# Two score blocks put side by side between matmuls of the second product, and one more tile of the first product in the values' buffers

## The chip, the cores and the metric

The kernel runs on one core of a Trainium2 chip. The metric is the device time of one execution in microseconds (us). Runs of this kernel differ among themselves by a few tenths of a microsecond.

## The reference

Attention with a few sink positions and a sliding window, followed by a two-layer network with a sigmoid-approximated gelu on the attention's output. Batch 4, 8 heads, 768 positions, 64 elements a head; 4 sinks, a window of 128; the network goes from 512 to 2048 and back to 512.

```python
scores = scale * np.matmul(q, k.transpose(0, 1, 3, 2))
keep = is_sink | in_window            # pos < n_sink, or 0 <= rel < window
scores = np.where(keep, scores, -1000000000.0)
scores = scores - np.max(scores, axis=-1, keepdims=True)
a = np.exp(scores)
a = a / (np.sum(a, axis=-1, keepdims=True) + 1e-09)
attn_out = np.matmul(a, v)
x = attn_out.transpose(0, 2, 1, 3).reshape(B * S, H * D)
h = x @ w_in
g = h * (1.0 / (1.0 + np.exp(-1.702 * h)))
out = g @ w_out
```

## The kernel before

**Tiles.** The 3072 rows of `x` are 12 groups of 256 (NG = 12, three to a batch entry). For a group, attention runs over four pairs of heads (hp = 0 to 3). The first product (`hidden`) makes the 2048 hidden features of a group in eight tiles (F2 = 0 to 7) of 256 features each, transposed, with 8 matmuls a tile; a gelu on ScalarE writes each into `gT`. The second product (`o`) makes a group's two blocks of 128 rows with 16 accumulating matmuls each.

**Attention of one group n.** `scores(n, hp)` writes the products of queries and keys (the previous 128 keys and the own 128, two heads, two blocks of rows) into a tile `nat`, with eight matmuls that use 64 rows of the array each. `maxima(n, hp)` on VectorE merges the two halves under the window's mask (L236), reduces to the row maximum (L240) and folds the sinks' maximum in (`bias`, L244). `weights` on ScalarE takes four exponentials (L255). `weights_transposed` turns them round: from group 3 on with a transposing DMA on the SP queue. `lower` (VectorE, L305) and `upper` (POOL, `affine_select`, L318) cut the transposed weights to the window; `values` multiplies with v into a tile `av`, and `normal` divides (L361, L362) into `xn`. The sinks have their own small path: `sinks`, `sink_terms` (L281, the tile `ts`), `sink_weights` (L290), `sink_transposed` (`tAs`, then the copy to `AsT`, L297). `x_transposed` turns `xn` to `xT` with a DMA.

**Accumulators.** All matmul results go to a pool with three tags. `nat` has two buffers, for scores. `mm` has two (`mm_bank`), for the hidden tiles `hT` and the `o` blocks. `av` has two (`av_bank`), for `tAs`, the sinks' scores `sk`, the values `av`, and hT of F2 = 2 and 3 in the one group g = NG - 2. Buffers of a tag are handed out in turn, and a tile waits until the tile two before it of the same tag has been read.

**The order.** The order on each engine is that of the program text (a manual schedule); each engine works its own queue in order and waits on semaphores. The loop at L665 runs n = 2 to 13, and one pass is called a stage here. In stage n, attention of group n is finished, the scores of group n + 1 begin, the first product runs for group n - 1 and the second for group n - 2. A stage first calls `second`, then goes through F2 = 0 to 7: after hT1 come `sink_transposed(n)`, the sinks and the first two pairs' scores and maxima of group n + 1 (`ahead`); after later tiles come the four `values` and `normal`.

In `second`, the first two pairs' weights go to ScalarE, then TensorE runs the first `o` block (16 matmuls), the third pair's scores, four matmuls of the second block, the fourth pair's scores, and the other twelve. `out_store(g2, 0)` copies the first block on ScalarE (L435), `out_store(g2, 1)` the second on VectorE (L437), and each store is issued on the SP queue (L439). VectorE's order in this part: third pair's maxima, fourth pair's maxima, `ts`, the L437 copy, then `lower` of the first pair, `AsT`, the sinks' values, and so on. SP's: the first two pairs' transposes, the first block's store, the third pair's transpose, the second block's store, the fourth pair's transpose, and the transpose of the queries and keys of group n + 2. POOL's: `upper` of the four pairs, with loads of group n + 3 issued between and after them; v's loads are paced by `rcp` tiles (`paced_load`).

Of the kernel before, what the change touches and what calls it, by code (L numbers as in the profile page):

```python
# [57 lines left out]
def kernel(  # L58
# [18 lines left out]
    NF = DF // P  # L77
    NT = S // TG
    NG = B * NT
# [23 lines left out]
    def mm_bank(name, shape=(P, 512), dt=FP32):  # L103
        return psp.tile(list(shape), dt, tag="mm", bufs=2, name=name)
# [66 lines left out]
    def sink_keys(b: int, copy):  # L171
        kT = G[b * NT]["qkT"]
        for h in range(2):
            copy(
                out=kd[b][bass.ts(h, D), :, bass.ts(h, n_sink)],
                in_=kT[bass.ts(h, D), 1, 0, :, 0:n_sink],
            )
# [31 lines left out]
    def scores(g: int, hp: int):  # L209

        b, t = divmod(g, NT)
        qkT = G[g]["qkT"]
        nat = psp.tile([P, 2, 2, 2 * P], FP32, tag="nat", bufs=2, name=f"nat{g}_{hp}")
        for i in range(2):
            I = 2 * t + i
            prev = None if I == 0 else qkT[:, 1, 0, hp] if i else G[g - 1]["qkT"][:, 1, 1, hp]
            for part, keys in ((0, prev), (1, qkT[:, 1, i, hp])):
                for h in range(2):
                    r = bass.ts(h, D)
                    o = nat[:, h, i, bass.ts(part, P)]  # L220
                    if keys is None:
                        nc.tensor.matmul(o, masked_l[r], masked_r[r], start=True, stop=True)
                    else:
                        nc.tensor.matmul(o, qkT[r, 0, i, hp], keys[r], start=True, stop=True)  # L224
        G[g]["nat", hp] = nat

    def kinds(mask, t: int):

        m = mask.rearrange("p (i c) -> p i c", i=2)
        if t == 0:  # L230
            return m.unsqueeze(1).broadcast_to((P, 2, 2, P))
        return m[:, 1:2].unsqueeze(1).broadcast_to((P, 2, 2, P))

    def maxima(g: int, hp: int):
        nat = G[g]["nat", hp]
        nc.vector.copy_predicated(  # L236
            out=nat[:, :, :, P:], mask=kinds(take_prev, g % NT), data=nat[:, :, :, 0:P]
        )
        m1 = work.tile([P, 2, 2], FP32, tag="m1", name=f"m1{g}_{hp}")
        nc.vector.tensor_reduce(  # L240
            out=m1.rearrange("p h i -> p (h i)"), in_=nat.rearrange("p h i c -> p (h i) c")[:, :, P:],
            axis=AX.X, op=ALU.max,
        )
        nc.vector.scalar_tensor_tensor(  # L244
            out=G[g]["bias"][:, :, hp], in0=m1.rearrange("p h i -> p i h"), scalar=-scale,
            in1=G[g]["m2"][:, :, hp], op0=ALU.mult, op1=ALU.min,
        )

    def weights(g: int, hp: int):

        nat, bias = G[g]["nat", hp], G[g]["bias"]
        A = work.tile([P, 4, P], FP16, tag="A", bufs=4, name=f"A{g}_{hp}")
        for h in range(2):
            for i in range(2):
                nc.scalar.activation(  # L255
                    out=A[:, 2 * h + i], in_=nat[:, h, i, P:], func=AF.Exp, bias=bias[:, i, hp, h : h + 1],
                    scale=scale,
                )
        G[g]["A", hp] = A

    def weights_transposed(g: int, hp: int):
        A = G[g]["A", hp]
        AT = work.tile([P, 2, 2, P], FP16, tag="AT", bufs=6, name=f"AT{g}_{hp}")
        flat = AT.rearrange("p h i s -> p (h i) s")
        if g < 3:
            bank = av_bank if g == 2 or (g, hp) == (1, 3) else mm_bank
            tp = bank(f"tA{g}_{hp}", (P, 4, P), FP16)
            for a in range(4):
                nc.tensor.transpose(tp[:, a], A[:, a], ident)
            if g == 0 or hp < (2 if g == 2 else 3):  # L270
                nc.scalar.copy(flat, tp)
            else:
                nc.vector.tensor_copy(out=flat, in_=tp)
        else:
            nc.sync.dma_start_transpose(flat, A.rearrange("p a c -> p (a c)"))
        G[g]["AT", hp] = AT
# [10 lines left out]
    def sink_weights(g: int):  # L287
        ts_ = G[g]["ts"]
        As = sinkA[g % 2]
        nc.scalar.activation(out=As[:, 0:64], in_=ts_.rearrange("p a j -> p (a j)"), func=AF.Exp)  # L290
        G[g]["As"] = As
# [92 lines left out]
    def hidden(g: int, F2: int):  # L384
        xT = G[g]["xT"]
        if F2 == 0:
            G[g]["gT"] = work.tile([P, NF, TG], FP16, tag="gT", bufs=3, name=f"gT{g}")

        bank = av_bank if g == NG - 2 and F2 in (2, 3) else mm_bank
        hT = bank(f"hT{g}_{F2}", (P, 2, 2, P))  # L390
        for f in range(2):
            F = 2 * F2 + f
            for c in range(4):
                nc.tensor.matmul(  # L394
                    hT[:, f], w_in16[:, c, bass.ts(F, P)], xT[:, :, c], start=(c == 0), stop=(c == 3)
                )
        nc.scalar.activation(  # L397
            out=G[g]["gT"][:, 2 * F2 : 2 * F2 + 2].rearrange("p f s -> p (f s)"),
            in_=hT.rearrange("p f i s -> p (f i s)"),
            func=AF.Gelu_apprx_sigmoid,  # L400
        )

    def out_part(g: int, i: int, part: int):

        if part == 0:
            G[g]["o", i] = mm_bank(f"o{g}_{i}")
        o, gT = G[g]["o", i], G[g]["gT"]
        for F in range(4 * part, 4 * part + 4):
            nc.tensor.matmul(o, gT[:, F, bass.ts(i, P)], w_out16[:, F], start=(F == 0), stop=(F == NF - 1))  # L409

    def out_last(g: int, i: int):

        b, t = divmod(g, NT)
        gT, r = G[g]["gT"], b * S + t * TG + i * P
        osb = work.tile([P, DM], FP32, tag="osb", bufs=3, name=f"osb{g}_{i}")
        for half in range(2):
            c = bass.ts(half, DM // 2)
            o = mm_bank(f"o{g}_{i}_{half}", (P, DM // 2))
            for F in range(NF):
                nc.tensor.matmul(o, gT[:, F, bass.ts(i, P)], w_out16[:, F, c], start=(F == 0), stop=(F == NF - 1))  # L420
            if half == 0:
                nc.scalar.copy(osb[:, c], o)
                nc.sync.dma_start(out[r : r + P, c], osb[:, c])
            else:
                d, a = bass.ts(2, P), bass.ts(3, P)
                nc.vector.tensor_copy(out=osb[:, d], in_=o[:, 0:P])
                nc.sync.dma_start(out[r : r + P, d], osb[:, d])
                nc.scalar.copy(osb[:, a], o[:, P:])
                nc.scalar.dma_start(out[r : r + P, a], osb[:, a])

    def out_store(g: int, i: int):
        b, t = divmod(g, NT)
        osb = work.tile([P, DM], FP32, tag="osb", bufs=3, name=f"osb{g}_{i}")
        if i == 0:
            nc.scalar.copy(osb, G[g]["o", i])  # L435
        else:
            nc.vector.tensor_copy(out=osb, in_=G[g]["o", i])  # L437
        r = b * S + t * TG + i * P
        nc.sync.dma_start(out[r : r + P, :], osb)  # L439
# [54 lines left out]
    def o(g: int, i: int, *parts):  # L494
        if 0 <= g < NG:
            for p in parts:
                out_part(g, i, p)

    def valued(g: int, hp: int):
        values(g, hp)  # L500
# [129 lines left out]
    def second(n: int, g2: int, att: bool):  # L630

        if att and n + 1 < NG and (n + 1) % NT == 0:
            sink_keys((n + 1) // NT, nc.gpsimd.tensor_copy)
        if att:
            for hp in (0, 1):
                weights(n, hp)
                weights_transposed(n, hp)
        o(g2, 0, 0, 1, 2, 3)
        if att:
            scores(n, 2)  # L640
            maxima(n, 2)
        if g2 == NG - 1:
            out_store(g2, 0)
            out_last(g2, 1)
            return
        o(g2, 1, 0)
        if att:
            scores(n, 3)
            maxima(n, 3)
            sink_terms(n)  # L650
        o(g2, 1, 1, 2, 3)
        out_store(g2, 0)
        if att:
            weights(n, 2)
            weights_transposed(n, 2)
        out_store(g2, 1)
        if att:
            weights(n, 3)
            weights_transposed(n, 3)
            sink_weights(n)  # L660
            lower(n, 0)
            if n + 2 < NG:
                transposed_qk(n + 2)

    for n in range(2, NG + LAG2):  # L665
        att = n < NG
        g1, g2 = n - LAG1, n - LAG2

        if n > 2:
            second(n, g2, att)  # L670
        else:
            transposed_qk(n + 2)
# [73 lines left out]
```

## Time and profile before

| what | value |
|---|---|
| median of 3 runs | 243.81 us (243.29 to 244.23) |
| the profiled execution | 243.37 us |
| its span, from the first to the last instruction | 241.5 us |
| busy: TensorE / VectorE / ScalarE / POOL | 222.7 / 146.1 / 156.1 / 104.7 us |
| granted TensorE clock over the span | 0.998 |

Stages of the profiled execution, each from its first `o` matmul:

| n | 2 | 3 | 4 | 5 | 6 | 7 | 8 | 9 | 10 | 11 | 12 | 13 |
|---|---|---|---|---|---|---|---|---|---|---|---|---|
| starts at, us | 43.57 | 62.70 | 79.56 | 96.84 | 114.63 | 131.46 | 148.74 | 166.12 | 182.94 | 200.59 | 216.90 | 230.92 |
| lasts, us | 19.1 | 16.9 | 17.3 | 17.8 | 16.8 | 17.3 | 17.4 | 16.8 | 17.7 | 16.3 | 14.0 | 10.6 |

Stages 3, 6 and 9 finish the first group of a batch entry, which has fewer matmuls in `values`. A row of the trace in order of time has the start in us from the span's start, the duration, engine, line, operation, output and inputs, shape, and a count of merged instructions; in brackets stands how long the engine was idle before it and what ended that. TensorE's durations include the time in its pipeline, so rows of matmuls overlap, and a step is better read from start to start. "DVE" is VectorE, "ACT" ScalarE, "PE" TensorE's matmuls, "PEld" its weight loads.

### The profile page before, as it was taken

How to read it: one execution, taken by the hardware profiler on the slowest of the kernel's cores; microseconds unless marked ns; L12 is line 12 of the kernel's file. 1: busy time of each engine (PE TensorE's matmuls, PEld its weight loads, DVE VectorE, ACT ScalarE, POOL GpSimd, SP SyncE). 2: the span in 40 equal slices, each digit the busy share in tenths (PEclk: the TensorE clock that was granted, in tenths of full speed). 3: DMA queues.
4: the chain of work that ended last, by engine and by line, in shares of the span. 5: the costliest groups of instructions: out<-in, count | busy, mean ns of one | idle time of the engine just before them, and what ended most of it. 6: DMA issues, size and time to landing. Idle time of an engine off the chain costs nothing.

```text
span 241.5 us, 5809 instructions
## 1 busy us (share of the span) xinstructions
PE 222.7 (92%) x2220; PEld 155.7 (64%) x2220; DVE 146.1 (61%) x389; ACT 156.1 (65%) x355; POOL 104.7 (43%) x158
## 2 busy tenths in 40 slices
PE   1656799999999999999999999999999999999994
PEld 0443678569658569478478487486585685684863
DVE  4688856488568378377667575586682893830100
ACT  2268693784866875785786776677668658760531
POOL 8977486847326447354438057058020310310000
PEclk9999999999999999999999999999999999999999
DMA  8999999999999999999999999999982513503102
GB/s 74 151 188 193 177 207 180 154 120 145 127 150 190 138 165 157 112 189 121 124 183 159 153 163 141 173 134 139 129 214 46 151 25 62 148 11 87 46 0 87
DMA packets 130699, 32.07 MB, mean 133 GB/s; under 512 B 123120, under 2 KB 127728, under 8 KB 130672
## 3 DMA queue, kind: packets, MB, share of 16 engines
q0 software_dynamic: 79104, 13.64, 78.9%
q1 hardware_dynamic: 50992, 17.88, 43.0%
q8 instruction: 17, 0.28, 0.5%
q10 hardware_dynamic: 576, 0.20, 0.3%
q14 instruction: 10, 0.08, 0.1%
HBM read 27.50 MB, written 6.29 MB: 140 GB/s over the span
## 4 chain that ended last, share of the span: by engine, by line
PE 63%; DVE 14%; ACT 13%; DMA 5%; issue 3%; POOL 1%; SPq 0%; ACTq 0%; DVEq 0%; POOLq 0%
PE hT L394 28%; PE o L409 22%; ACT A L255 6%; DVE m L240 5%; DVE nat L236 5%; ACT L397 3%; PE nat L224 3%; DMA AT<-A 2%; PE av L344 2%; DMA qkn<-in_k_dram 2%; ACT gT L397 2%; PE av L332 2%; PE av L340 2%; PE o L420 1%; DVE xn L362 1%
## 5 line engine op out<-in xcount | busy, mean ns | idle before, releaser
L394 PE MATMUL hT<-xT,w_in 128*128 128x256 f16 x768 | 95.1, 274 | 1.1 <-ACT gT L397 0.4
L409 PE MATMUL o<-w_out,gT 128*128 128x512 f16 x368 | 85.4, 380 | 0.0
L397 ACT ACTIVATE gT<-hT 128x512 f16<-128x512 f32 x96 | 56.1, 597 | 41.2 <-PE hT L394 40.9
L394 PEld LDWEIGHTS <-w_in 128*128 128x128 f16 x768 | 72.7, 98 | 13.4 <-issue 0.6
L318 POOL TENSOR_SCALAR_AFFINE_SELECT up<-AT 128x512 f16<-128x512 f16 (+1 forms) x48 | 27.8, 585 | 99.1 <-DMA AT<-A 91.7
L255 ACT ACTIVATE A<-nat,bias 128x128 f16<-128x128 f32 x192 | 53.7, 376 | 18.6 <-DVE bias L244 17.1
L409 PEld LDWEIGHTS <-gT 128*128 128x128 f16 x368 | 33.6, 98 | 37.2
L236 DVE COPY_PREDICATED nat<-prev,nat 128x512 f32<-128x512 uint16 x48 | 33.2, 692 | 28.7 <-PE nat L224 19.0
L240 DVE TENSOR_REDUCE m<-nat 128x4 f32<-128x512 f32 x48 | 33.2, 691 | 1.7
L123 POOL DMA_DIRECT2D vn<-in_v_dram x24 | 21.3, 898 | 3.4 <-DMA w_out<-in_moe_w_out_dram 2.3
L123 POOL DMA_DIRECT2D qkn<-in_k_dram x24 | 21.3, 894 | 2.5 <-DMA w_in<-in_moe_w_in_dram 2.0
L123 POOL DMA_DIRECT2D qkn<-in_q_dram x24 | 21.6, 910 | 1.3 <-POOLq L727 0.8
L305 DVE TENSOR_TENSOR lo<-AT,own 128x512 f16<-128x512 f16 (+1 forms) x48 | 18.2, 397 | 5.9 <-DMA AT<-A 5.7
L362 DVE TENSOR_TENSOR xn<-av,rcp 128x256 f16<-128x256 f32 x48 | 20.4, 424 | 1.7
L340 PE MATMUL av<-vn,up 128*128 128x65 f16 x160 | 18.4, 196 | 0.0
L344 PE MATMUL av<-vn,lo 128*128 128x65 f16 x160 | 18.3, 196 | 0.0
L332 PE MATMUL av<-vs,AsT 128*128 128x130 f16 x80 | 16.5, 224 | 0.6 <-DVE xn L362 0.3
L224 PEld LDWEIGHTS <-qkT 64*128 64x128 f16 x352 | 11.8, 100 | 7.7 <-issue 7.0
L224 PE MATMUL nat<-qkT 64*128 64x128 f16 x288 | 16.6, 232 | 0.0
L361 DVE RECIPROCAL rcp<-av 128x4 f32<-128x4 f32 x48 | 8.5, 178 | 12.3 <-PE av L344 12.0
L340 PEld LDWEIGHTS <-up 128*128 128x128 f16 x160 | 14.8, 100 | 1.4 <-POOL up L318 0.5
L397 ACT ACT_TABLE_LOAD x11 | 14.1, 1283 | 0.2
(58 smaller groups left out, 180.3 us busy)
## 6 DMA issues: line engine op xcount, KB each, us to landing
out_dram<-osb SPq DMA_DIRECT2D x23, 256.0 KB
qkn<-in_q_dram POOLq DMA_DIRECT2D x24, 128.0 KB, 5.6
qkn<-in_k_dram POOLq DMA_DIRECT2D x24, 128.0 KB, 5.4
vn<-in_v_dram POOLq DMA_DIRECT2D x24, 128.0 KB, 6.6
w_in<-in_moe_w_in_dram POOLq DMA_DIRECT2D x4, 512.0 KB, 10.4
w_out<-in_moe_w_out_dram POOLq DMA_DIRECT2D x4, 512.0 KB, 11.6
AT<-A SPq DMA_TRANSPOSE x36
xT<-xn SPq DMA_TRANSPOSE x10
```

What stands on the lines that cost most here:

```text
L123: nc.gpsimd.dma_start(dst, (q, k, v)[e][b, :, rows].rearrange("h s d -> s h d"))
L224: nc.tensor.matmul(o, qkT[r, 0, i, hp], keys[r], start=True, stop=True)
L236: nc.vector.copy_predicated(out=nat[:, :, :, P:], mask=kinds(take_prev, g % NT), data=nat[:, :, :, 0:P])
L240: nc.vector.tensor_reduce(out=m1.rearrange("p h i -> p (h i)"), in_=nat.rearrange("p h i c -> p (h i) c")[:, :, P:], axis=AX.X, op=ALU.max,)
L255: nc.scalar.activation(out=A[:, 2 * h + i], in_=nat[:, h, i, P:], func=AF.Exp, bias=bias[:, i, hp, h : h + 1], scale=scale,)
L318: nc.gpsimd.affine_select(out=out, in_=in_, pattern=[[0, rows], [-1, P]], compare_op=ALU.is_gt, fill=zero_reg, base=0, channel_multiplier=1,)
L340: nc.tensor.matmul(av[:, i, h], up[:, h, i], vn[b][J // 2][:, J % 2, head], start=False, stop=False)
L344: nc.tensor.matmul(av[:, i, h], own_w[:, h, i], vn[b][t][:, i, head], start=(I == 0), stop=(I == 0 or h == 1))
L362: nc.vector.tensor_tensor(out=G[g]["xn"][:, :, hp], in0=av[:, :, :, 0:D], in1=rcp.to_broadcast((P, 2, 2, D)), op=ALU.mult)
L394: nc.tensor.matmul(hT[:, f], w_in16[:, c, bass.ts(F, P)], xT[:, :, c], start=(c == 0), stop=(c == 3))
L397: nc.scalar.activation(out=G[g]["gT"][:, 2 * F2 : 2 * F2 + 2].rearrange("p f s -> p (f s)"), in_=hT.rearrange("p f i s -> p (f i s)"), fun ...
L409: nc.tensor.matmul(o, gT[:, F, bass.ts(i, P)], w_out16[:, F], start=(F == 0), stop=(F == NF - 1))
```

## The change

In `second`, both score blocks of the third and fourth pair now stand together, after the first two matmuls of the second `o` block; both maxima and `sink_terms` follow, then the other 14 matmuls. `out_part` takes a range of the 16 matmuls in place of a quarter, and the helper `o` is adapted to it. In `hidden`, the third tile (F2 = 2) of groups 2 to 9 (first product in stages 3 to 10) takes an `av` buffer, as F2 = 2 and 3 of group 10 did before and still do.

```diff
-        bank = av_bank if g == NG - 2 and F2 in (2, 3) else mm_bank
+        more = (2,) if 2 <= g < NG - 2 else (2, 3) if g == NG - 2 else ()
+        bank = av_bank if F2 in more else mm_bank
...
-    def out_part(g: int, i: int, part: int):
+    def out_part(g: int, i: int, F0: int, F1: int):
-        if part == 0:
+        if F0 == 0:
             G[g]["o", i] = mm_bank(f"o{g}_{i}")
         o, gT = G[g]["o", i], G[g]["gT"]
-        for F in range(4 * part, 4 * part + 4):
+        for F in range(F0, F1):
             nc.tensor.matmul(o, gT[:, F, bass.ts(i, P)], w_out16[:, F], start=(F == 0), stop=(F == NF - 1))
...
-                out_part(g, i, p)
+                out_part(g, i, 4 * p, 4 * p + 4)
...
         o(g2, 0, 0, 1, 2, 3)
-        if att:
-            scores(n, 2)
-            maxima(n, 2)
         if g2 == NG - 1:
             out_store(g2, 0)
             out_last(g2, 1)
             return
-        o(g2, 1, 0)
+        out_part(g2, 1, 0, 2)
         if att:
+            scores(n, 2)
             scores(n, 3)
+            maxima(n, 2)
             maxima(n, 3)
             sink_terms(n)
-        o(g2, 1, 1, 2, 3)
+        out_part(g2, 1, 2, NF)
         out_store(g2, 0)
```

## The prediction

> **What bounds the kernel now.** I read the page first, then the busy time by stage (a stage is one pass of the loop at L665, named by its n; it starts with the first `o` matmul of `second`), then the chain of waits through stage 6, then the rows of that stage in order of time.
>
> ```profile
> span 241.5 us, 5809 instructions
> PE 222.7 (92%) x2220; PEld 155.7 (64%) x2220; DVE 146.1 (61%) x389; ACT 156.1 (65%) x355; POOL 104.7 (43%) x158
> ...
> PE 63%; DVE 14%; ACT 13%; DMA 5%; issue 3%; POOL 1%; SPq 0%; ACTq 0%; DVEq 0%; POOLq 0%
> ```
>
> TensorE is the bound, but a fourth of the chain that ended last goes through VectorE and ScalarE. By stage (length, busy time of PE, PEld, DVE, ACT, POOL):
>
> ```profile
> 96.84:114.63 17.79, 17.37 (x183) 11.91 (x180) 11.46 (x29) 12.30 (x29) 8.02 (x13) 1.00 1.56 141
> 114.63:131.46 16.83, 16.75 (x171) 11.47 (x169) 11.67 (x30) 12.19 (x29) 9.19 (x17) 1.00 1.48 155
> ```
>
> The clock is full (1.00). Stage 6 (second row) is nearly all TensorE; stage 5 has 0.4 us of plain idle. Its detour, in the chain of waits (start, length, what):
>
> ```profile
> 114.79 3.45 PE o L409 x16
> ...
> 118.69 0.71 DVE nat L236
> 119.42 0.70 DVE m L240
> ...
> 120.23 0.70 DVE nat L236
> 120.95 0.70 DVE m L240
> ...
> 122.02 1.14 ACT A L255 x4
> ...
> 123.32 1.28 ACT L397
> 124.61 0.60 ACT gT L397
> ...
> 125.26 1.91 PE hT L394 x16
> ```
>
> The third pair's scores start two maxima on VectorE, the fourth pair's weights, a table load and the first gelu on ScalarE; the third tile of the first product (hT2) waits for that gelu, since it takes hT0's buffer. The same stretch in order of time:
>
> ```profile
> 118.18 0.23 PE L222 MATMUL nat<-maskedr,maskedl 64*128 64x128 f16 x2
> ...
> 118.51 1.04 PE L409 MATMUL o<-w_out,gT 128*128 128x512 f16 x4
> ...
> 119.48 0.23 PE L222 MATMUL nat<-maskedr,maskedl 64*128 64x128 f16 x2
> ...
> 119.81 2.77 PE L409 MATMUL o<-w_out,gT 128*128 128x512 f16 x12
> ...
> 121.88 0.23 DVE L281 TENSOR_TENSOR ts<-bias,sn 128x64 f32<-128x64 f32 x1
> ...
> 122.41 1.98 PE L394 MATMUL hT<-xT,w_in 128*128 128x256 f16 x16
> ...
> 122.61 0.69 DVE L437 COPY osb<-o 128x512 f32<-128x512 f32 x1 [0.51 <-PE o L409]
> ```
>
> A busy PE hides small losses, so I take steps from start to start in the single records. An `o` matmul steps 0.213 (twelve of them: 122.41 - 119.81 = 2.60), a set of eight 64-row score matmuls 0.21. On top, going from `o` to scores costs 0.10 and going back 0.12, twice a stage. hT1 waits 0.07 for L437 to end (123.30), since it takes that buffer; hT2 comes 0.27 after its step, of which 0.12 is the way back from scores and 0.15 the wait for the gelu (end 125.21, start 125.26). In stage 10 that wait is 0.51.
>
> **Part 1: the scores side by side.** Nothing is added or left out: 16 score matmuls, two maxima and 32 `o` matmuls stay. One round trip between `o` and scores goes: 0.10 + 0.12 = 0.22 on TensorE. Two sets with nothing between them show no gap in the rows of `ahead` (sets start at 124.56 and 124.79). But the third set now comes behind two matmuls of the second `o`: 2 x 0.213 = 0.43 later. Queued behind it on VectorE, in order: both maxima, `ts` and the L437 copy. VectorE idled 2.08 before the first maxima and runs without a gap from 118.69 to the end of `ts` at 122.11, so the fourth pair's maxima gain nothing from earlier scores and the whole run moves by 0.43: `ts` at 122.31 to 122.54. L437 doesn't depend on `ts`; independent neighbours on VectorE overlap by 0.08 (bias ends 120.32, the next nat starts 120.23), so it runs 122.46 to 123.15. It was bound by TensorE before (0.51 idle), by VectorE after. hT1 can start at 123.19; TensorE is there at 122.41 - 0.22 + 0.85 = 123.04 and waits 0.15 instead of 0.07. Of the 0.22, 0.16 reaches hT1 (123.35 before).
>
> The fourth set needs its `nat` buffer from weights(n, 1), whose last exponential ends 3.92 to 4.04 after the stage's start; the set comes at 3.55 + 0.43 + 0.21 = 4.19. No wait, with 0.10 to spare after 0.05 for the signal. ScalarE's weights move by 0.43, covered by its idle 1.46 and 0.39, and with them the SP queue: the third pair's transpose is issued at 7.49 instead of 7.06 into the stage, read by VectorE at 13.8; the fourth pair's, held by the output store before it on SP (issued 8.70, then 0.43), stays at 9.1, since the weights then end at 8.98. The store itself follows L437, 0.16 earlier. POOL's `up` of the third pair (9.7 to 10.5) may come some tenths later; its reader on TensorE is at 15.5.
>
> **Part 2: the third tile in a buffer of the values.** In stages 3 to 10 hT2 takes the `av` buffer that `AsT`'s copy frees, and waits for that (0.25 after `tAs`, before the scores end) in place of the gelu. It starts 0.12 after the scores: 10.48 - 0.16 = 10.32 into the stage instead of 10.63, a gain of 0.31. The first gelu is what is late next: 0.43 later it ends at 11.01, and hT3, which now takes hT0's buffer, comes at 10.32 + 0.85 = 11.17. So the cover is 0.12; a gelu later than that is paid in full. Stage 11 has this edit already.
>
> **What takes it back.** (a) The values. The fourth pair's `lo` stands before the first `rcp` and `xn` on VectorE, and the third `av` waits for that `xn`. Stage 5, where the transposed weights landed late:
>
> ```profile
> 112.02 0.43 DVE L305 TENSOR_TENSOR lo<-AT,own 128x512 f16<-128x512 f16 x1 [0.93 <-DMA AT<-A]
> ...
> 113.05 0.22 PE L332 MATMUL av<-vs,AsT 128*128 128x130 f16 x1 [0.34 <-DVE xn L362]
> ```
>
> From landing to `av` takes 113.05 - 112.02 = 1.03. With TensorE 0.31 earlier, `av` is wanted at 15.39 of the stage, so a landing after 14.37 costs its whole excess. Landings seen: 15.18 (stage 5), 14.77 (8), 14.34 (7), no wait in the others. Stages 5 and 8 thus gain 0.
>
> (b) VectorE can be held up by POOL:
>
> ```profile
> 207.72 0.63 POOL L318 TENSOR_SCALAR_AFFINE_SELECT up<-AT 128x512 f16<-128x512 f16 x1 [0.95 <-DMA AT<-A]
> ...
> 207.84 0.59 DVE L281 TENSOR_TENSOR ts<-bias,sn 128x64 f32<-128x64 f32 x1
> ```
>
> This `ts` took 0.59 instead of 0.23 and ended with the `up`. `ts`, `bias` and `lo` show this in 12 places, L437, nat and m in none. With `ts` at 7.67 to 7.90 of the stage, it meets the first `up`, which starts at 7.69, 7.80, 7.65 and 7.88 in stages 4, 5, 7 and 8. If `up` starts first, L437 moves by about 0.44 and that stage loses 0.13 instead of gaining 0.31. Stages 4 and 7 are nearest: one of the two, 0.18 between them, I take.
>
> The Trainium skill (SBUF — State Buffer, "Who interferes with whom") says that a VectorE instruction with two SBUF inputs contends with a GpSimd instruction that reads SBUF, and that whoever issues first blocks the other. The 0.59 row agrees; by this rule the delay of `ts` is a risk in every stage where an `up` starts near it, which rival 2 prices from rows.
>
> In stage 10, `up` at 5.63 to 6.26 meets the moved second-last `bias` (5.94; +0.17), while the 0.36 that the next `bias` lost before (189.99, 0.53 long) goes: hT2 at 10.50 instead of 10.99, 0.49 gained. In stage 11 both `bias` meet an `up` (+0.10, +0.21) less the 0.36 of `ts`: 0.
>
> **Sum.** Stages 3, 6, 9: 0.93. Stages 4 and 7: 0.18. Stages 5, 8 and 11: 0. Stage 10: 0.49. Together 1.6. The profiled execution took 243.37 (span 241.5 and 1.9 around it), 0.44 under the median 243.81; so 241.8 for it and 242.2 for the median.
>
> **Rivals.**
> 1. The late landings of 5 and 8 were chance: they gain 0.31 each like the others, `up` meets no `ts`, and stage 5's 0.51 stall goes. 1.6 + 0.62 + 0.44 + 0.5 = 3.2: 240.6; with half of it, 241.3. For: transfers of `q` (issued 8.97 and 9.05 in those stages) went just ahead of the transpose (9.14, 9.13), a matter of tenths. Against: three of nine stages show it.
> 2. `up` comes first in stages 4, 5, 7 and 8: 0.93 + 0.49 - 4 x 0.13 = 0.9 gained, 242.9. Against: the `up`s of 5 and 8 start well after `ts` begins.
> 3. Slower: the fourth pair's transposed weights land as late as 15.18 in stages 4 to 8, because transfers now stand closer together. `av` then comes at 16.21 instead of 15.70, 16.21, 15.47, 15.70 and 15.80: 0.51 + 0 + 0.74 + 0.51 + 0.41 = 2.2 lost, against 0.62 + 0.49 gained in 3, 9 and 10: 1.1 slower, 244.9. It decides from 14.37 on. For: stage 5. Against: the transpose is issued no later than before.
> 4. The change doesn't do what it says: the fourth set waits 0.2 for its `nat` buffer (cover 0.10). L437 then starts 0.1 later, nine times: 0.9 less, 243.1.
>
> **Chances.** Forecast 0.42; rival 1 0.24; rival 2 0.13; rival 3 0.13; rival 4 0.08. About 0.5% (1.2 us) is what a measurement of this kernel can tell from no change: faster needs under 242.6. The forecast gives 0.37 of its chance to that, rival 1 all, rivals 2 and 4 some 0.02 together: 0.63. Slower by over 1.2 is the half of rival 3 and what I can't see: 0.12. The rest, 0.25, is between. The range leaves out the far end of rival 1 and most of rival 3: 240.7 to 244.1.
>
> **What would show it.** Right: one pair of ways into and out of scores in `second`; the first maxima at 4.49 of the stage; L437 at 7.8 without idle time; hT2 0.12 after the last score set; stages 3, 6 and 9 shorter by 0.3. Wrong: hT3 waiting for the gelu, L437 starting after 8.2, `av` waiting for `xn` in more than stages 5 and 8, or an `up` side that stops TensorE.

## The result and the profile after

The changed kernel takes 242.24 us (median of 21 runs, 241.02 to 244.12), the kernel before 243.71 us (21 runs, 242.58 to 245.38). The ratio is 0.9944, with a 95% interval from 0.9925 to 0.9963: 1.5 us less between the medians. The forecast was 242.2. Single runs of one kernel spread over about 3 us here, not over the few tenths named at the start, so medians and intervals have to carry a difference of this size.

The page of the profiled execution (243.37 us before, span 241.5):

```profile
span 240.3 us, 5809 instructions
PE 220.8 (92%) x2220; PEld 155.9 (65%) x2220; DVE 145.3 (60%) x389; ACT 155.3 (65%) x355; POOL 104.4 (43%) x158
...
PE 78%; DVE 9%; DMA 5%; ACT 3%; issue 2%; POOL 1%; DVEq 0%; POOLq 0%
```

VectorE's and ScalarE's share of the chain that ended last fell from 27% to 12%. The busy time by stage, stages 4 to 7 and 9 (first to last time, length, then busy time of PE, PEld, DVE, ACT and POOL, and last the granted clock, the DMA engines' share and GB/s):

```profile
79.09:96.07 16.98, 16.98 (x182) 11.93 (x180) 11.08 (x29) 12.32 (x29) 8.67 (x14) 1.00 1.39 156
96.07:113.06 16.99, 16.99 (x183) 11.95 (x181) 11.32 (x29) 12.21 (x29) 10.01 (x18) 1.00 1.35 146
113.06:131.52 18.46, 16.57 (x170) 11.39 (x168) 11.67 (x30) 12.29 (x29) 7.99 (x15) 1.00 1.78 164
131.52:148.72 17.20, 17.03 (x183) 11.96 (x180) 11.20 (x29) 12.32 (x29) 8.06 (x13) 1.00 1.21 149
...
165.78:182.30 16.52, 16.52 (x170) 11.47 (x168) 11.68 (x30) 12.08 (x29) 4.46 (x9) 1.00 1.17 145
```

Against 17.28, 17.79, 16.83, 17.28 and 16.82 before, every one is shorter by 0.1 to 0.8, but for stage 6, which is 1.6 longer. Stages 3 to 11 together take 153.08 instead of 154.20. Stage 9 shows the change undisturbed. Its chain of waits (start, length, what) no longer leaves TensorE:

```profile
165.94 3.88 PE o L411 x18
169.83 0.16 PE nat L222 x2
169.99 0.17 PE nat L224 x6
170.16 0.06 PE nat L222 x2
170.21 0.17 PE nat L224 x6
170.38 3.13 PE o L411 x14
173.51 1.86 PE hT L396 x16
175.37 0.06 PE tAs L295
175.43 0.18 PE sk L195 x8
175.61 0.55 PE nat L224 x16
176.16 1.85 PE hT L396 x16
```

The detour over maxima, exponentials, a table load and the first gelu is gone. The same stage in order of time:

```profile
170.27 0.70 DVE L236 COPY_PREDICATED nat<-prev,nat 128x512 f32<-128x512 uint16 x1 [2.52 <-ACT osb L437]
...
173.46 0.23 DVE L281 TENSOR_TENSOR ts<-bias,sn 128x64 f32<-128x64 f32 x1
...
173.60 0.68 DVE L439 COPY osb<-o 128x512 f32<-128x512 f32 x1
...
176.09 1.37 PE L396 MATMUL hT<-xT,w_in 128*128 128x256 f16 x11
176.19 1.58 ACT L399 ACTIVATE gT<-hT 128x512 f16<-128x512 f32 x3
```

The stage starts at 165.78. The first maxima comes at 4.49 of it (4.06 before), the copy follows `ts` without a gap, and hT2 starts at 10.31, ahead of the first gelu (10.41). In stage 6 TensorE then waits for something else:

```profile
122.67 1.05 PE L396 MATMUL hT<-xT,w_in 128*128 128x256 f16 x8 [1.89 <-DMA xT<-xn]
```

The transposed `xT`, issued 0.88 into the stage, is there only at 9.6. It is wanted at 7.57, and was wanted at 7.78 before. The trace keeps 16 marks for the landing of such a transfer: here eight come at 7.80 to 7.88 of the stage and eight at 9.43 to 9.57. Between them, from 7.97 to 9.45, lies a pause of the transfers, in which 21 packets take 1.45 to 1.55 us each (the last section has more on pauses). In a second profile of this kernel (below) the same `xT` has landed at 5.88.

### The profile page after: what moved, and what is told of

Its sections match the earlier page's. It is cut to its first block, busy times and chain, and to the rows that moved or that the text cites. A ratio compares the mean times of both kernels' runs of the same rounds, so it can differ in the third digit from the quotient of the medians.

```text
span 240.3 us, 5809 instructions
## 1 busy us (share of the span) xinstructions
PE 220.8 (92%) x2220; PEld 155.9 (65%) x2220; DVE 145.3 (60%) x389; ACT 155.3 (65%) x355; POOL 104.4 (43%) x158
## 4 chain that ended last, share of the span: by engine, by line
PE 78%; DVE 9%; DMA 5%; ACT 3%; issue 2%; POOL 1%; DVEq 0%; POOLq 0%
PE hT L396 35%; PE o L411 27%; PE nat L224 4%; DMA xT<-xn 4%; DVE m L240 3%; DVE nat L236 3%; PE av L344 2%; ACT A L255 2%; PE av L340 2%; PE av L332 2%; DMA qkn<-in_k_dram 2%; PE tA L269 2%; PE o L422 1%; DVE xn L362 1%; PE tqk L152 1%
## 5 line engine op out<-in xcount | busy, mean ns | idle before, releaser
L411 PE MATMUL o<-w_out,gT 128*128 128x512 f16 x368 | 83.8, 379 | 0.0
L399 ACT ACTIVATE gT<-hT 128x512 f16<-128x512 f32 x96 | 55.4, 597 | 37.0 <-PE hT L396 36.8
L411 PEld LDWEIGHTS <-gT 128*128 128x128 f16 x368 | 34.3, 98 | 38.4
L224 PE MATMUL nat<-qkT 64*128 64x128 f16 x288 | 15.5, 232 | 0.0
```

The lines of the kernel that those rows point to most:

```text
L399: nc.scalar.activation(out=G[g]["gT"][:, 2 * F2 : 2 * F2 + 2].rearrange("p f s -> p (f s)"), in_=hT.rearrange("p f i s -> p (f i s)"), fun ...
```

## The experiments

All ratios are to the kernel before, run on the same chip, with 95% intervals.

### The parts apart: the scores' place alone, the third tile's buffer alone

```diff
 # side_only: the changed kernel, but
-        more = (2,) if 2 <= g < NG - 2 else (2, 3) if g == NG - 2 else ()
+        more = (2, 3) if g == NG - 2 else ()
 # buffer_only: the kernel before, but
-        bank = av_bank if g == NG - 2 and F2 in (2, 3) else mm_bank
+        more = (2,) if 2 <= g < NG - 2 else (2, 3) if g == NG - 2 else ()
+        bank = av_bank if F2 in more else mm_bank
```

> The scores stand side by side as in the changed kernel, but the third tile of the first product stays in an mm buffer. Theory (scores later by two o matmuls move VectorE's run and the first gelu by 0.43, and this tile waits for that gelu): the tile starts at 11.06 of the stage instead of 10.63 before, so 0.43 more in each of stages 3 to 9, 0.2 in stage 10, partly given back where a late landing made TensorE wait anyway; about 2.5 us slower than before, ratio 1.008 to 1.013. Rival (the saved way between o and scores, 0.16 to 0.22 a stage, is a gain by itself): 1.4 to 2.0 us faster, ratio about 0.993.

Measured: 247.54 us, ratio 1.0149 (1.0119 to 1.018), slower than either kernel. The mechanism is the one expected, in order of time (stage 6, starting at 116.56):

```profile
126.97 1.08 ACT L399 ACTIVATE gT<-hT 128x512 f16<-128x512 f32 x2
127.62 0.60 PE L396 MATMUL hT<-xT,w_in 128*128 128x256 f16 x4 [0.68 <-ACT gT L399]
```

hT2 waits for the gelu and starts at 11.06, to the hundredth as expected. The size was too small: in stages 4, 5, 8 and 10 an `up` on POOL held VectorE up as well, and hT2 came at 11.23 to 11.42.

> The scores stay where they were before; only the third tile of the first product of stages 3 to 10 takes an av buffer. Theory: the tile starts at 10.48 of the stage, 0.12 after the scores, instead of 10.63; 0.15 less in seven stages and 0.51 in stage 10, 1.6 us in all without late landings and 1.2 with them, ratio 0.993 to 0.996. Its profile shows no wait for the gelu. Rival (this buffer only passes the wait on to the next tile or the values): no change, ratio 0.998 to 1.002.

Measured: 242.04 us, ratio 0.993 (0.9902 to 0.9958). In order of time, stage 9 (starting at 165.57; line numbers are one lower than in the changed kernel):

```profile
175.55 1.09 ACT L398 ACTIVATE gT<-hT 128x512 f16<-128x512 f32 x2
...
176.05 1.16 PE L395 MATMUL hT<-xT,w_in 128*128 128x256 f16 x9
```

hT2 starts at 10.48, before the first of the two gelus ends (10.58), so the rival falls. And again, beside the changed kernel:

> The third tile's buffer alone. Theory (late transfers and hold-ups take from the side-by-side scores what they save): within 0.6 us of the changed kernel, ratio 0.992 to 0.996. Rival (the scores' place is worth 1.4 us with loads too): 243.6 us, ratio 0.999.

> The changed kernel, beside the two that follow. Theory: 242.2 us, ratio 0.994; its stages without a late transfer or a hold-up by POOL last 16.52 and 16.98.

Measured: the buffer alone 242.14 us, 0.9931 (0.9912 to 0.995); both parts 242.19 us, 0.9941 (0.9921 to 0.9961). hT2 starts at 10.48 with the buffer alone, undisturbed stages last 16.69 and 17.15, with both parts 16.52 and 16.98. The scores' place thus saves 0.17 in each undisturbed stage (0.11 in stage 11), 1.5 over nine stages, and nothing that the medians show. In the profiles, what stages 3 to 11 last beyond their undisturbed length is 2.4 and 2.2 us with both parts (two executions), and 0.7 and 1.3 with the buffer alone. Split by the rows, late transfers make 2.0 and 0.6 of it with both parts and 0.7 and 1.3 with the buffer alone. Hold-ups of VectorE by POOL make 0.4 and 1.5 with both parts, and 0 and 0.06 with the buffer alone.

One such loss in the second profile of the changed kernel, stage 4 (starting at 79.33), in order of time:

```profile
86.98 1.22 POOL L318 TENSOR_SCALAR_AFFINE_SELECT up<-AT 128x512 f16<-128x512 f16 x2 [5.49 <-DMA AT<-A]
87.01 0.67 DVE L281 TENSOR_TENSOR ts<-bias,sn 128x64 f32<-128x64 f32 x1
87.61 0.68 DVE L439 COPY osb<-o 128x512 f32<-128x512 f32 x1
...
88.34 0.38 PE L396 MATMUL hT<-xT,w_in 128*128 128x256 f16 x2 [0.40 <-DVE osb L439]
```

The first `up` starts 0.03 before `ts`; `ts` takes 0.67 instead of 0.23, the copy is late, and hT1 starts at 9.01 of the stage instead of 8.56. In stage 7 `bias` and `ts` are both held up (0.63 and 0.61 long, hT1 at 9.41), and in stages 5 and 8 the third `av` waits 0.11 and 0.46 for late `lo`.

### The scores later still

```diff
-        out_part(g2, 1, 0, 2)
+        out_part(g2, 1, 0, 4)
...
-        out_part(g2, 1, 2, NF)
+        out_part(g2, 1, 4, NF)
```

> The changed kernel with four instead of two matmuls of the second o block ahead of the two score blocks. TensorE does the same work with the same number of ways into and out of scores. Theory (VectorE's run from the first scores to the copy of the second o block sets when the second tile may start): the run moves by another 0.43, the copy starts at 8.25 of the stage, the second tile at 8.98 instead of 8.55 and the third at 10.75; about 0.43 a stage, 3.4 us slower than the changed kernel where nothing else is late, 1 us slower than the kernel before, ratio 1.002 to 1.007. Rival (only the number of ways between o and scores counts): as the changed kernel, ratio 0.994.

Measured: 246.13 us, ratio 1.0104 (1.0067 to 1.0141). In order of time, stage 6 (starting at 115.61):

```profile
123.72 0.23 DVE L281 TENSOR_TENSOR ts<-bias,sn 128x64 f32<-128x64 f32 x1
...
123.86 0.68 DVE L439 COPY osb<-o 128x512 f32<-128x512 f32 x1
124.59 0.60 PE L396 MATMUL hT<-xT,w_in 128*128 128x256 f16 x4 [0.38 <-DVE osb L439]
```

The copy at 8.25, hT1 at 8.99: VectorE's run decides, and the rival falls. The loss is above the range, since `ts` or a `bias` now meets an `up` in stages 4, 7, 8 and 11 (hT1 at 9.28 to 9.80).

### The copy ahead of `ts`

```diff
             maxima(n, 3)
-            sink_terms(n)
         out_part(g2, 1, 2, NF)
...
         out_store(g2, 1)
         if att:
+            sink_terms(n)
             weights(n, 3)
```

> The changed kernel with VectorE's copy of the second o block ahead of the tile ts. Theory: the copy starts at 7.76 of the stage, when o is done, instead of 7.82 and is no longer moved where POOL holds up ts; the second tile starts at 8.49 instead of 8.55; 0.06 in nine stages, 0.5 us less than the changed kernel, ratio to before about 0.992. Rival (the loss in these stages is late transfers, not VectorE): no difference from the changed kernel, 0.994.

> The changed kernel with the copy of the second o block ahead of ts. Theory: 0.5 to 1.0 us below the changed kernel, ratio 0.990 to 0.992. Rival (the first run of it was lucky with its transfers): as the changed kernel, 0.994.

Measured: 241.19 us, ratio 0.9909 (0.9875 to 0.9944), and 241.72 us, 0.9916 (0.9901 to 0.9932), the second beside 242.19 for the changed kernel. In order of time, stage 6 of the first:

```profile
121.49 0.16 DVE L244 SCALAR_TENSOR_TENSOR bias<-m,m 128x4 f32<-128x4 f32 x1
...
121.78 0.69 DVE L439 COPY osb<-o 128x512 f32<-128x512 f32 x1
122.38 0.22 DVE L281 TENSOR_TENSOR ts<-bias,sn 128x64 f32<-128x64 f32 x1
```

The copy has 0.13 of idle time ahead of it again: TensorE sets it. hT1 starts at 8.51 in 17 of 18 stages of the two profiles. Each interval overlaps that of the changed kernel, but the median was lower each time, by about what was expected. By its medians it is the best version found, with 0.8 to 0.9% off the kernel before. That it beats the buffer alone isn't shown: those intervals overlap too. Late transfers stay: in its second profile stages 7 and 8 still lose 0.7 and 1.4 to the fourth pair's weights.

### Without loads in the loop

```diff
+        if g >= 6:
+            G[g]["qkn"] = G[g - 3]["qkn"]
+            return
...
-    vn = [[big.tile(...) for t in range(NT)] for b in range(B)]
+    vn = [[big.tile(...) for t in range(NT)] for b in range(2)] * 2
```

> The kernel before without the loads of q, k and v for groups 6 to 11, which use those of groups 3 to 5 again (v: of the first two batch entries), so no load runs in stages 3 to 11; the pacing copies stay. It is the base for the next run. Both theories: no waits for late transposed weights, stages of 16.8 and 17.3 apart from VectorE's hold-ups by POOL; ratio 0.990 to 0.998.

> The changed kernel with the same loads left out. Theory (0.3 a stage is really saved on TensorE, and what isn't seen of it with loads is given back to transposed weights and xT that land late and to POOL's hold-ups): 2.6 to 3.5 us less than the kernel before without loads, against 1.5 us with loads; stages 3, 6 and 9 last 16.5. Rival (the change saves only what the medians show): 1.2 to 1.8 us less.

> Only the third tile moved to an av buffer, scores as before, and the loads of groups 6 to 11 left out as in the two runs without loads. Theory (side by side, the way saved between o and scores is worth 0.17 in stages 3, 6 and 9, but nearly nothing in the stages in which the moved bias meets the first up, and 0.1 in stage 11): 241.8 us, 0.5 to 0.9 above the changed kernel without loads (241.15), stages of 16.69 and 17.15. Rival (side by side is worth 0.17 in each of nine stages as soon as no transfer is late): 242.6 or more.

Measured: 244.52 us (ratio 1.0024, 1.0001 to 1.0048), 241.15 us (0.9888, 0.9868 to 0.9908) and 241.6 us (0.991, 0.9893 to 0.9928). Without loads the change is worth 3.4 us, of which the third tile's buffer makes 2.9 and the scores' place 0.45. The 0.45 is not clear of noise: the run with the buffer alone was in another round, and the two intervals overlap. In the profiles without loads, every stage of the buffer alone has its undisturbed length, and with both parts 0.7 is lost, nearly all of it to hold-ups (hT1 at 8.61 to 8.72 in stages 4, 5, 7, 8 and 10). That supports late transfers and hold-ups as what takes the rest. It holds in sum, not transfer by transfer, and part of the 3.4 is new: the kernel before got no faster without its loads, against both theories, and against the kernel before with its loads (243.86) the gain is 2.7. Its stage 7 in order of time (starting at 131.77; line numbers are three higher here):

```profile
138.68 0.64 POOL L321 TENSOR_SCALAR_AFFINE_SELECT up<-AT 128x512 f16<-128x512 f16 x1 [0.66 <-DMA AT<-A]
138.81 0.52 DVE L247 SCALAR_TENSOR_TENSOR bias<-m,m 128x4 f32<-128x4 f32 x1
...
142.10 1.08 ACT L400 ACTIVATE gT<-hT 128x512 f16<-128x512 f32 x2
142.75 0.38 PE L397 MATMUL hT<-xT,w_in 128*128 128x256 f16 x2 [0.43 <-ACT gT L400]
```

The transposed weights land sooner, so `up` runs sooner, and now meets a `bias` in all six stages from 5 to 10, the fourth pair's in 5, 7, 8 and 10 and the third pair's in 6 and 9: 0.41 to 0.56 instead of 0.16. The gelu is late by as much, and hT2 starts at 10.87 to 11.02 instead of 10.63. With the buffer that gelu has a cover, and the hold-up is free; with the scores' place too, VectorE's run is what hT1 waits for, and it isn't.

### The fourth pair's transpose ahead of the store

On the SP queue the second block's store is issued after the fourth pair's transpose; the copy stays where it is. `out_store` then returns the call that issues the store. The first of the two runs below has the copy ahead of `ts` as well, the second the old order of scores and `ts`.

```diff
-        out_store(g2, 1)
+        store = out_store(g2, 1, False)
         if att:
             weights(n, 3)
             weights_transposed(n, 3)
+        store()
+        if att:
             sink_weights(n)
```

> The changed kernel with the copy of the second o block ahead of ts, and on the SP queue the fourth pair's transpose ahead of the second block's output store instead of behind it. Theory (the transpose lands late because 256 KB of output and the loads of q move ahead of it): it is issued at 9.0 of the stage and lands a microsecond earlier, the values no longer wait for it, the 0.5 us stalls of stages 5 and 8 go; 0.5 to 1.2 us less than with the copy ahead alone, ratio 0.986 to 0.989. Rival (its lateness comes from the loads and from pauses of the transfers, not from the store): as with the copy ahead alone, 0.991.

> The scores as before, the third tile in an av buffer, and the fourth pair's transpose ahead of the second block's output store on the SP queue, with the copy and ts in their old order. Theory (side-by-side scores save 0.16 a stage, which late transposes took back): with the transposes early the gap to the run with side-by-side scores opens, this one is 0.8 to 1.5 us slower than that; ratio 0.991 to 0.993, stages of 16.7 and 17.15. Rival (the scores' place is worth nothing in the end): the two runs are equal.

Measured: 241.94 us, 0.9905 (0.9863 to 0.9947), and 241.57 us, 0.9918 (0.9893 to 0.9944). The first is no better than the copy ahead alone by its median, as the rival said. Its runs spread from 239.72 to 244.19, and the interval just reaches the ratio that the theory gave, so the rows have to decide. The SP queue did change, here in stage 6 with the third and fourth pair's transposes merged:

```profile
121.54 2.72 SPq L275 DMA_TRANSPOSE AT<-A  x2
124.35 0.54 SPq L441 DMA_DIRECT2D out_dram<-osb  x1
```

The transpose is issued 0.4 earlier, at 9.0 of the stage. By its landing marks it took 5.48 and 5.61 us in stages 5 and 8, against 5.43 and 5.51 in the first run with the copy ahead alone, where the store goes first, and in the other stages from 6 to 10 it differs by no more than 0.1. The third `av` still waits 0.17 and 0.33 in stages 5 and 8. Stage 4, where it took 2.50 instead of 4.55, loses 0.49 to a late `xT`. So in the late stages the store is not what makes the fourth pair's weights late. The marks of all 14 profiles point to loads and pauses together (last section). The second run neither opened the gap nor settled the scores' worth: its profiled execution was its slowest (243.08).

## Why the prediction was right

- **The removed way between `o` and scores**: right. One pair of steps of 0.10 and 0.12 is left in `second`, and hT0 starts at 7.57 of the stage instead of 7.78.
- **VectorE's run moved by 0.43, the copy bound by it**: right to a hundredth. `ts` at 7.68 to 7.90, the copy to 8.50, hT1 waiting 0.12 (forecast 0.15). The later-scores run shows the cause: another 0.43 there is another 0.43 for hT1.
- **The fourth set finds its `nat` buffer free**: right. Sixteen score matmuls run without a gap from 3.98 on; the rival of a wait there falls.
- **The third tile freed from the gelu, hT3 covered by 0.12**: right. hT2 at 10.31 (forecast 10.32), gelu end 11.01 (11.01), hT3 at 11.20 (11.17).
- **Single stages**: stages 3 and 9 gained 0.33 and 0.30 (forecast 0.31), stage 10 0.50 (0.49) through the moved `bias` that was named, stage 11 0.11 (0).
- **Hold-ups by POOL, one of stages 4 and 7**: right in kind. In the first profile stage 7 (`bias` 0.38 instead of 0.16, the second `up` and not the first), in the second both. There the two lost 0.21 and 0.56 against before, where the forecast had 0.13 for a stage so hit.
- **Late landings: stages 5 and 8 gain nothing**: this step was wrong as put, and rival 1 was nearer: stage 5 gained 0.81 and stage 8 0.32 in the first profile. In the kernel before, a pause had fallen between issue and landing in both stages; in the changed kernel neither profile had one in stage 5. The loss fell on stage 6 and on `xT`, a transfer that the forecast never named. Without the 1.95 lost there, stages 3 to 11 would have gained 3.1, close to the 3.2 of rival 1. In the second profile stage 8 had a late landing again. The amount came out near (1.12 and 1.38 gained in the two profiles, 1.5 between the medians, against 1.6), the places didn't, so that the number is right is partly luck.
- **What the forecast left unsaid**: it shared 0.31 a stage between both parts and took losses off the whole. The hold-ups belong to one part, while late transfers hit either version. The buffer alone took 1.7 and 1.8 us off in its two comparisons, as much as both parts (1.5 and 1.7); the scores' place puts VectorE's run on the way to hT1 and so exposes TensorE to every hold-up there. The rule of the Trainium skill (SBUF — State Buffer, "Who interferes with whom") that a VectorE instruction with two SBUF inputs and a GpSimd instruction that reads SBUF block one another is what the 0.67 and 0.52 rows show, on a longer list of victims than `ts`: `bias` too.
- **Slower** (rival 3): did not happen; no profile shows late weights in all of stages 4 to 8.

## What to carry to other kernels

Before two edits are taken as one gain, price each alone: here one was worth the whole and the other 0.17 in an undisturbed stage and nothing that the medians show. An edit that saves time on the bound engine by delaying a run on another can move that run onto the path, and from then on each hold-up of it counts; look for what can be taken out of the run (`ts`) or put behind the instruction that frees the buffer. And a stall in one profile is a place where a transfer may be late, not a place where it is: sum such losses over the execution.

## What the runs showed of the hardware

- Fewer transfers did not make the kernel before faster: without six groups' loads it took 244.5 us against 243.9 (ratio 1.0001 to 1.0048), since POOL's work came earlier and held up VectorE's `bias` (0.41 to 0.56 instead of 0.16). The two versions with the third tile's buffer did get faster.
- The packet records of the executions with all loads show pauses, five to eight of them, in which packets under way that else take 0.02 to 0.09 us take 1.1 to 2.2 us. Most of these packets are the SP queue's, in some pauses the loads', and fewer others end meanwhile (24 in the pause at 121.0, against 478 in the 1.2 us before it). In the changed kernel they lie at 65.5, 82.6, 121.0, 134.7, 161.0 and 172.7 us; that of 121.0 is the one with the late `xT`. The kernel before without its loads had three, the changed one four. Counted from 0.8 us on, all 14 profiles have one at 159 to 166 us and ten have one at 108 to 112 us; in the kernel before these two fall in stages 8 and 5. Their cause wasn't tried.
- The fourth pair's transpose (128 x 512, f16), from its issue to its last landing mark, in stages 3 to 11 of the 14 profiles: 2.4 to 2.6 us in 45 of 53 cases with neither a load of q, k or v nor a pause on the way (4.0 to 4.4 in the other eight, all in stage 11); 2.4 to 5.4 with a load (51 cases, median 3.6); 4.0 to 4.2 with a pause alone (four cases); 3.9 to 6.3 with both (18 cases, median 5.5). These are rows put side by side, not a run that changes one thing.
